# An attention and mixer kernel: three operations of the first steps moved, and one product put into another pair of banks

## The chip, the cores and the metric

The kernel runs on one core of a Trainium2 chip. A core has five engines that run side by side, each with its own queue of instructions taken in order: TensorE (PE in the profile: matrix products, with PEld for the loading of weights), VectorE (DVE), ScalarE (ACT), GpSimd (POOL) and SyncE (SP, which here only issues transfers). They wait for each other through semaphores. SBUF is the core's working memory, PSUM the memory that TensorE writes: eight banks of 2 KB in each of 128 partitions, used here in pairs. The metric is the device time of one execution, in microseconds (us).

## The reference

Linear attention with a decay for each head, in blocks of 64 positions, and then a mixing layer of low rank over the positions and a pair of large products over the channels. There are 4 batches, 8 heads, 768 positions, heads of 64 channels, hence 512 channels; the rank is 32 and the hidden width 2048.

```
for b in range(nb):                       # blocks of 64 positions
    intra = einsum('bhic,bhjc->bhij', qb, kb) * Dmask
    intra = einsum('bhij,bhjd->bhid', intra, vb)
    inter = einsum('bhid,bhde->bhie', qb * lam_pow, kv_state)
    out[:, :, sl] = intra + inter
    kv_state = lam_block * kv_state + einsum('bhsd,bhse->bhde', kb * rev_pow, vb)
x = out laid out as (batch, position, head * channel)
u = x + ((x^T U) V)^T                     # mixing over the 768 positions
result = u + relu(u @ w_ch1) @ w_ch2
```

q, k, v and lam come as 32-bit floating numbers. The four weights U, V, w_ch1 and w_ch2 come as 64-bit ones, and the kernel turns them into 32-bit ones on the chip, from pairs of 32-bit words. Its products that need more than one pass of TensorE use split operands: a high part, and what is left over (a low part).

## The kernel before

**Tiling.** The attention takes 128 positions at a time, all 8 heads at once: 6 such tiles for each of 4 batches, so 24 steps, s = 0 to 23, with c = s % 6 the tile's place in its batch. Behind them come the large products (from about 113 us), which hold most of the time; the change does not touch them.

**A step**, by the names of its parts, with the engine and line of each:

- `prep(s)`: TensorE turns q and k over (L419) into the pair of banks `pqk`, ScalarE copies them out as `qt` and `kt` (L425).
- `scale(s)`: GpSimd makes `qs`, q with its decay (L450), and then `ks` of the following step (L439).
- `scores(s)`: q by k on TensorE (L466), into `pss`.
- `masked(s)`: VectorE multiplies the scores by the mask of decays into `sm`, in two operations (L475).
- `intra(s)`: `sm` by v on TensorE (L524), into the pair `px`. Its first half waits for the first mask operation, the second half for the second.
- `inter(s)`: `qs` by the running state `kv` (L536), into the same `px`.
- `state(s)`: `ks` by v on TensorE (L489) into a part of a pair of banks that is called `pkv`; VectorE then makes the next state `kv` from it, by a copy at c = 0 (L495), and elsewhere by adding the faded old state (L497), which `fade(s)` made on ScalarE (L459).
- `take_x(s)`: ScalarE copies `px` out (L546), which frees `px`. There is one pair `px`, so the next step's first product into it waits for that.
- `next_v`, `next_k` and the loads in `prep` issue the loads of later tiles; `next_v` stands on ScalarE's queue.
- behind the sixth step of a batch, `low(b)` multiplies x by U (L556), `low_rows` splits the result into high and low parts, on VectorE (L589, L597) and GpSimd (L598), and four transfers on SyncE's queue exchange halves of it (L608).
- a batch later, `mix(s)` multiplies by V (L631) into the pair `pm`, `mixed(s)` adds the result to x on VectorE (L643), `turn` turns x over into the other columns of `pm` (L694), and ScalarE, VectorE and GpSimd split it for the large products (L708, L709, L701).

The pairs of banks are `pm`, `pss`, `pqk` and `px`: eight banks, all taken. A tile that goes into a pair waits until what was there before has been read.

**Order.** The order is written out by hand: one list `pieces` of (part, step), each part issuing its instructions on the queues of its engines, in the order of the list. On each engine the instructions run in that order. `aside(s)` is the place in step s at which the conversions of the weights stand; which of them stand there says the table that assigns the steps of `u_side`, `v_steps()` and `w1_steps` to places. `aside_first` says whether `aside(s)` stands ahead of `masked(s + 1)` or behind it. What a conversion has to do on ScalarE is kept back to the place `late`, in the following step.

**The conversions** of U and of V run through the same steps. `one`: VectorE takes out the exponent (L170) and the mantissa (L158), and ScalarE makes the scale from the exponent (L177, L178). `two`: the low word is added (L188). `three` and `four`: the sign is put in and the two are multiplied (L196, L201). For V there follow `five`, the high part (L788, and copies on ScalarE, L795), and `low`, the low parts of its rows: group 3 on GpSimd and group 1 on VectorE (L799). Each `low` is two operations, one for each half of the columns, 32 partitions by 384. At `aside(3)`, in the fourth step, stand the last two operations of U (L196, L201) and the first of V (L170, L158). At `aside(6)`, in the seventh step and behind `masked(7)`, stand both operations of V's low part on VectorE.

Of the kernel before, what the change touches and what calls it, by code (L numbers as in the profile page):

```python
# [18 lines left out]
def kernel(  # L19
# [28 lines left out]
    nc = tc.nc  # L48
# [3 lines left out]
    NT = S // P  # L52
# [36 lines left out]
    def on_scalar(what):  # L89
        if late and late[0] is None:  # L90
            late.append(what)
        else:
            what()
# [216 lines left out]
    def two_banks(name, tag):  # L310
        return psf.tile([P, 2, N], FP32, tag=tag, name=name)
# [7 lines left out]
    def bank(shape, name, tag):  # L319
        return psa[0].tile(shape, FP32, tag=tag, bufs=2, name=name)  # L320
# [5 lines left out]
    def parts(s):  # L326
        return 2 if s == 0 else 1
# [67 lines left out]
    half = [slice(0, D), slice(D, P)]  # L395
# [81 lines left out]
    def state(s):  # L477
        c = s % NT
        if c < NT - 1:
            ks, vr = st[s]["ks"], raw[s, "v"]  # L480
            if c == 0 and s > NT:
                pkv = st[s]["px"][:, 0, HP * D : 2 * HP * D]
            else:
                tag = "pm" if s <= NT else "pss" if c > 1 else "pqk"
                pkv = two_banks("pkv", tag)[:, 0, 0 : HP * D]
            pkv = pkv.rearrange("p (a e) -> p a e", a=HP)
            for a in range(HP):
                for x in range(2):
                    nc.tensor.matmul(  # L489
                        out=pkv[half[x], a, :], lhsT=ks[:, a, x, :], rhs=vr[:, 2 * a + x, :],  # L490
                        start=True, stop=True,
                    )
            kv[s + 1] = att.tile([P, HP, D], FP32, tag="kv", bufs=2, name="kv")
            if c == 0:
                nc.vector.tensor_copy(out=kv[s + 1], in_=pkv)  # L495
            elif "faded" in st[s]:
                nc.vector.tensor_tensor(out=kv[s + 1], in0=pkv, in1=st[s]["faded"], op=ALU.add)  # L497
            else:
                for a in range(HP):
                    nc.vector.scalar_tensor_tensor(  # L500
                        kv[s + 1][:, a, :], kv[s][:, a, :], lamc[:, a, :], pkv[:, a, :],
                        ALU.mult, ALU.add,
                    )
# [47 lines left out]
    def low(b):  # L551

        pp = two_banks("pp", "px")[:, 0, 0:P] if b < B - 1 else bank([P, P], "pp", "b2")
        for c in range(NT):
            for g in range(G):
                nc.tensor.matmul(  # L556
                    out=pp[g * R : (g + 1) * R, :], lhsT=u_w[:, c, :],
                    rhs=xs[b * NT + c][:, g * P : (g + 1) * P],
                    start=(c == 0), stop=(c == NT - 1),
                )  # L560
        pps[b] = pp
# [156 lines left out]
    for s in range(NS):  # L718
        b, c = divmod(s, NT)
        done = s - NT - 1  # L720
        more = s + 1 < NS
        turns = done > 0 and (done - 1) // TG < FG
        mixes = 0 <= done < NS - NT - 1
        rows = c == 0 and b > 0
        step = [("fade", s)] * (c > 0)
        step += [("mix", done)] * (mixes and c != 1) + [("turn", done - 1)] * turns
        step += [("next_of_low", b - 1)] * rows
        step += [("split", done - 1)] * turns
        step += [("prep", s + 1)] * more
        step += [("mix", done + 1)] * (not more)  # L730
        step += [("scale", s + 1)] * more
        step += [("mixed", done)] * (mixes and c != 1)
        step += [("late", s - 1)] * (1 < s < NT - 1 or s > NT)
        step += [("turned", done - 2)] * (done > 1 and c == 1)
        step += [("mixed", done + 1)] * (not more)
        both = [("intra", s), ("state", s)] 
        if s in inter_first:
            step += [("inter", s)] + both + [("next_v", s)]
        else:
            step += (both if s > NT else both[::-1]) + [("next_v", s), ("inter", s)]  # L740
        step += [("take_x", s)]
        step += [("next_of_low", b - 1)] * rows
        step += [("late", s)] * (s < 2 or s in (NT - 1, NT))
        step += [("turned", done - 1)] * (done > 0 and c > 0)
        step += [("mix", done), ("mixed", done)] * (mixes and c == 1)
        step += [("scores", s + 1)] * more
        step += [("low", b)] * (more and c == NT - 1)
        aside_first = 0 < s < NT - 2 or s > NT and c > 0
        step += [("aside", s)] * aside_first
        step += [("masked", s + 1)] * more  # L750
        step += [("low_rows", b)] * (more and c == NT - 1)
        step += [("aside", s)] * (not aside_first)
        step += [("store", done)] * (done >= 0 and done // TG < FG)
        step += [("next_k", s)] * (s > 0)
        pieces += step
    waiting = {name: list(range(NS)) for name in "qkv"}

    def load_next(name, engine=nc.sync):
        if waiting[name]:
            load(name, waiting[name].pop(0), engine)  # L760


    run = {
        "prep": prep, "fade": fade, "scores": scores, "masked": masked, "inter": inter, "take_x": take_x,
        "intra": intra, "state": state,
        "low": low, "low_rows": low_rows, "next_of_low": next_of_low, "mix": mix, "turn": turn,
        "mixed": mixed, "store": store, "next_v": next_v, "split": lambda s: splits.pop(s)(),
        
        "next_k": lambda s: load_next("k"), "third_v": lambda s: load_next("v", nc.scalar), "scale": scale, "turned": lambda s: turned.pop(s)(),
    }  # L770
    def v_steps():

        st = {}

        def dst():
            if "v" not in st:
                st["v"] = wconv.tile([P, C], FP32, tag="wf", name="vf")[0 : 2 * R, 0:SH]
            return st["v"]

        def parts(gs):  # L780
            for half in range(2):
                rows, cols = slice(half * R, (half + 1) * R), slice(half * SH, (half + 1) * SH)
                for g in gs:
                    yield v_hl[g * R : (g + 1) * R, cols], rows

        def five():
            st["t"] = t = wconv.tile([P, C], FP32, tag="wt", name="vt")[0 : 2 * R, 0:SH]
            nc.vector.tensor_scalar(  # L788
                t.bitcast(U32), st["v"].bitcast(U32), HI, None, ALU.bitwise_and
            )  # L790
            on_scalar(high)

        def high():
            for out, rows in parts((0, 2)):
                nc.scalar.copy(out, st["t"][rows])  # L795

        def low(g, engine):
            for out, rows in parts((g,)):
                engine.tensor_tensor(  # L799
                    out=out, in0=st["v"][rows], in1=st["t"][rows], op=ALU.subtract  # L800
                )

        halves = [moe_V[:, half * SH : (half + 1) * SH] for half in range(2)]
        return weight_steps(dst, halves, SH, 2 * R, in_parts=True) + [
            five, lambda: low(3, nc.gpsimd), lambda: low(1, nc.vector),
        ]


    u_side = weight_steps(
# [2 lines left out]
    side = {}  # L812
    for steps, at in (
        (u_side, (-1, 2, 2, 3, 3)),
        (v_steps(), (1, 1, 3, 4, 4, 4, 4, 5, 6)),
        (w1_steps(0, True, True), (8, 9, 10, 11, 12, 14, 15, 16, 17, 17, 20, 21)),
        (w1_steps(1, True, True), (14, 15, 16, 17, 18, 22, 23, NS, NS, NS, NS, NS)),
    ):
        assert len(steps) == len(at)
        for step, n in zip(steps, at):  # L820
            side.setdefault(n, []).append(step)
# [631 lines left out]
    for i in range(FT - EARLY, len(steps) - STAG):  # L1453
        g, ft = steps[i]
# [49 lines left out]
```

## Time and profile before

The time before is 637.38 us, the median of three runs (637.07 to 637.69).

| What | Value |
| --- | --- |
| time of the profiled execution | 637.08 us |
| its span, first to last instruction | 635.3 us |
| TensorE busy | 627.3 us, 99% |
| VectorE busy | 467.6 us, 74% |
| ScalarE busy | 330.9 us, 52% |
| GpSimd busy | 146.9 us, 23% |
| mean granted TensorE clock | 0.999 |

The page of the profile gives the busy time of each engine and "the chain of work that ended last", followed back from the last instruction to whatever released it, with the share of each engine. Other views of the same trace are used: the waits (which engine waited for which, in us, how many times, and the longest), and the timeline (start in us, duration in us, engine, line, operation, what it writes and reads, how many instructions the row merges, and in brackets the idle time before it and what ended it). A wait for several things is put down to the one that came last, and a name in brackets can be that of an engine that had long been done.

### The profile page before, as it was taken

How to read it: one execution, taken by the hardware profiler on the slowest of the kernel's cores; microseconds unless marked ns; L12 is line 12 of the kernel's file. 1: busy time of each engine (PE TensorE's matmuls, PEld its weight loads, DVE VectorE, ACT ScalarE, POOL GpSimd, SP SyncE). 2: the span in 40 equal slices, each digit the busy share in tenths (PEclk: the TensorE clock that was granted, in tenths of full speed). 3: DMA queues.
4: the chain of work that ended last, by engine and by line, in shares of the span. 5: the costliest groups of instructions: out<-in, count | busy, mean ns of one | idle time of the engine just before them, and what ended most of it. 6: DMA issues, size and time to landing. Idle time of an engine off the chain costs nothing.

```text
span 635.3 us, 13669 instructions
## 1 busy us (share of the span) xinstructions
PE 627.3 (99%) x5213; PEld 529.2 (83%) x5213; DVE 467.6 (74%) x752; ACT 330.9 (52%) x604; POOL 146.9 (23%) x125
## 2 busy tenths in 40 slices
PE   9999999999999999999999999999999999999997
PEld 8888989888888888888888888888888888888886
DVE  5776887757888788797888799784665754855844
ACT  4675756546777777778777744332322322323220
POOL 4476878000000000000667500030210300300300
PEclk9999999999999999999999999999999999999999
DMA  9989995348797888755876796363353353542521
GB/s 223 254 215 253 249 247 153 133 166 289 284 348 270 309 292 291 272 199 187 262 231 212 239 323 217 116 232 100 108 208 99 137 195 100 190 128 96 183 84 66
DMA packets 141955, 129.61 MB, mean 204 GB/s; under 512 B 82562, under 2 KB 99970, under 8 KB 141890
## 3 DMA queue, kind: packets, MB, share of 16 engines
q1 hardware_dynamic: 116768, 122.32, 59.6%
q10 hardware_dynamic: 25122, 6.42, 4.5%
q8 instruction: 41, 0.67, 0.4%
q14 instruction: 24, 0.20, 0.1%
HBM read 79.04 MB, written 49.28 MB: 202 GB/s over the span
## 4 chain that ended last, share of the span: by engine, by line
PE 97%; DVE 1%; ACT 1%; DMA 1%; issue 0%; ACTq 0%; DVEq 0%
PE pz L983 24%; PE pz L1343 14%; PE pz L1345 14%; PE pd L1347 14%; PE z L983 5%; PE pss L466 4%; PE px L524 4%; PE p L983 3%; PE pz L911 2%; PE d L983 2%; PE px L536 2%; PE pqk L419 2%; PE c L983 2%; PE pkv L489 1%; PE pd L922 1%; PE pp L556 1%
## 5 line engine op out<-in xcount | busy, mean ns | idle before, releaser
L1319 ACT ACTIVATE m<-rm 128x512 fp32r<-128x512 f32 x96 | 60.6, 631 | 174.0 <-PE pd L1347 131.0
L1324 DVE SCALAR_TENSOR_TENSOR m<-rm,m 128x512 fp32r<-128x512 f32 x96 | 71.6, 747 | 81.0 <-ACT m L1319 81.0
L983 PE MATMUL pz<-u_hl,w 128*128 128x512 f32 x448 | 110.3, 389 | 0.0
L1343 PE MATMUL pz<-w_hl,m 128*128 128x512 f32 x264 | 102.7, 389 | 0.0
L1345 PE MATMUL pz<-w_hl,m 128*128 128x512 f32 x264 | 102.7, 389 | 0.0
L1347 PE MATMUL pd<-w_d,m 128*128 128x512 f32 (+1 forms) x267 | 101.4, 387 | 0.0
L983 PEld LDWEIGHTS pz<-u_hl,w 128*128 128x128 f32 x448 | 84.1, 188 | 17.5
L285 POOL TENSOR_TENSOR w<-w 128x512 fp32r<-128x512 f32 x29 | 40.5, 1414 | 210.8 <-DVE w L279 197.3
L1325 DVE SCALAR_TENSOR_TENSOR m<-m 128x512 fp32r<-128x512 f32 x96 | 74.9, 780 | 3.1
L1375 POOL TENSOR_TENSOR o<-o,u 128x512 f32<-128x512 f32 x20 | 29.8, 1521 | 198.5 <-DVE o L1371 198.5
L983 PE MATMUL pz<-u_d,w 128*128 128x512 f32 x224 | 59.9, 389 | 0.0
L1347 PEld LDWEIGHTS pd<-w_d,m 128*128 128x128 f32 x267 | 49.8, 188 | 10.3
L1345 PEld LDWEIGHTS pz<-w_hl,m 128*128 128x128 f32 x264 | 49.6, 188 | 10.3
L1343 PEld LDWEIGHTS pz<-w_hl,m 128*128 128x128 f32 x264 | 49.6, 188 | 10.2
L983 PEld LDWEIGHTS pz<-u_d,w 128*128 128x128 f32 x224 | 42.0, 188 | 8.7
L1343 PE MATMUL pz<-w,m 128*128 128x512 f32 x120 | 46.7, 389 | 0.0
L1345 PE MATMUL pz<-w,m 128*128 128x512 f32 x120 | 46.7, 389 | 0.0
L1347 PE MATMUL pd<-w,m 128*128 128x512 f32 x120 | 46.7, 389 | 0.0
L990 ACT ACTIVATE pz<-pz 128x512 f32<-128x512 f32 x56 | 32.5, 581 | 26.4 <-PE pz L983 26.4
L475 DVE TENSOR_TENSOR sm<-pss,mask 128x512 f32<-128x512 f32 x48 | 30.9, 685 | 18.7 <-PE pss L466 18.4
L994 ACT ACTIVATE r<-pz 128x512 f32<-128x512 f32 x56 | 33.2, 595 | 12.1 <-PE pz L983 11.4
L196 DVE SCALAR_TENSOR_TENSOR sc<-words,sc 128x512 uint32<-128x512 uint32 (+2 forms) x34 | 23.7, 696 | 18.0 <-ACT sc L178 18.0
(140 smaller groups left out, 1119.8 us busy)
## 6 DMA issues: line engine op xcount, KB each, us to landing
r_d<-r SPq DMA_DIRECT2D x96, 256.0 KB, 2.9
rm<-r_d SPq DMA_DIRECT2D x96, 256.0 KB, 2.6
words<-in_moe_w_ch_dram SPq DMA_DIRECT2D x30, 512.0 KB, 5.1
wf<-forms_d SPq DMA_DIRECT2D x56, 128.0 KB, 2.9
u_d<-x_nat SPq DMA_DIRECT2D x24, 256.0 KB, 3.8
u<-u_d SPq DMA_DIRECT2D x24, 256.0 KB, 4.9
qraw<-in_q_dram SPq DMA_DIRECT2D x23, 256.0 KB, 5.0
out_dram<-o SPq DMA_DIRECT2D x23, 256.0 KB, 2.0
```

Source lines behind the costliest of these rows:

```text
L285: engine.tensor_tensor(out=st["third"], in0=st["low"].bitcast(FP32), in1=st["hi"].bitcast(FP32), op=ALU.subtract,)
L475: nc.vector.tensor_tensor(out=sm[:, x], in0=pss[:, x], in1=mask[:, x], op=ALU.mult)
L983: nc.tensor.matmul(out=out, lhsT=weights, rhs=moving, start=start and i == 0, stop=i == len(pieces) - 1, skip_group_check=not start,)
L990: nc.scalar.mul(acc, acc, 1.0 + E)
L994: nc.scalar.mul(r, acc, 4096.0)
L1319: nc.scalar.activation(out=m[:, 0], in_=rs[i], func=AF.Relu, scale=NEAR)
L1324: nc.vector.scalar_tensor_tensor(m[:, 1], r, 0.0, hi, ALU.max, ALU.subtract)
L1325: nc.vector.scalar_tensor_tensor(m[:, 2], hi, E, low, ALU.mult, ALU.subtract)
L1343: nc.tensor.matmul(out=pz, lhsT=m[:, 0, cols], rhs=hi, start=first, stop=False)
L1345: nc.tensor.matmul(out=pz, lhsT=m[:, 1, cols], rhs=low, start=False, stop=end)
L1347: nc.tensor.matmul(out=pd[:, part], lhsT=m[:, 2, cols], rhs=third[:, part], start=first, stop=end, skip_group_check=part.stop != C,)
L1375: nc.gpsimd.tensor_tensor(out=o, in0=o, in1=u, op=ALU.add)
```

## The change

Four edits.

- `aside_first` no longer holds for s = 3. In the fourth step U's last two operations and V's first two on VectorE stand behind `masked(4)`, no longer ahead of it.
- V's low part on VectorE is split. Its first operation, for the first half of the columns, stands in the seventh step (s = 6) behind `state(6)`, so ahead of `masked(7)`; the second stays at `aside(6)`, behind `masked(7)`.
- In the eighth step (s = 7) `state(7)` is issued ahead of `intra(7)`, not behind it.
- `state(7)` writes into the pair `pm`, which `mix(0)` takes next, no longer into `pqk`.

```diff
-                tag = "pm" if s <= NT else "pss" if c > 1 else "pqk"
+                tag = "pm" if s <= NT + 1 else "pss" if c > 1 else "pqk"
...
-        both = [("intra", s), ("state", s)] 
+        both = [("intra", s), ("state", s)] + [("v_low", s)] * (s == NT)
...
-            step += (both if s > NT else both[::-1]) + [("next_v", s), ("inter", s)]
+            step += (both if s > NT + 1 else both[1:] + both[:1]) + [("next_v", s), ("inter", s)]
...
-        aside_first = 0 < s < NT - 2 or s > NT and c > 0
+        aside_first = 0 < s < NT - 3 or s > NT and c > 0
...
-        def low(g, engine):
-            for out, rows in parts((g,)):
+        def low(g, engine, half=slice(0, 2)):
+            for out, rows in list(parts((g,)))[half]:
...
-            five, lambda: low(3, nc.gpsimd), lambda: low(1, nc.vector),
+            five, lambda: v_low.append(lambda: low(1, nc.vector, slice(0, 1))),
+            lambda: low(3, nc.gpsimd), lambda: low(1, nc.vector, slice(1, 2)),
...
+    v_low = []
+    run["v_low"] = lambda s: v_low.pop()()
...
-        (v_steps(), (1, 1, 3, 4, 4, 4, 4, 5, 6)),
+        (v_steps(), (1, 1, 3, 4, 4, 4, 4, 5, 5, 6)),
```

NT is 6, the number of tiles in a batch. No instruction is added or removed on any engine, and on ScalarE, GpSimd and SyncE the order stays as it was.

## The prediction, made before the changed kernel ran

> **What bounds the kernel now.** I read the page's chain first, then TensorE's waits, then the timeline of steps 2 to 8, engine beside engine. Steps are counted from s = 0: the "fourth step" is s = 3, the "eighth" is s = 7, and kv(s) is the state that inter(s) reads.
>
> The chain that ended last:
>
> ```profile
> PE 97%; DVE 1%; ACT 1%; DMA 1%; issue 0%; ACTq 0%; DVEq 0%
> ```
>
> TensorE is the path, so an edit is worth what it takes from TensorE's waits. These are the ones inside the attention steps (us in total, times, longest):
>
> ```profile
> PE px L524 <- issue: 1.1, 3, 0.6
> ...
> PE px L524 <- ACT qt L425: 0.7, 1, 0.7
> ...
> PE pm L631 <- DVE x_nat L643: 0.3, 1, 0.3
> ```
>
> The second is intra(4) at 25.44 us. The third is mix(1) at 41.44. Of the first, 0.35 us stands before intra(7) at 37.28. They add up to 1.3 us, 0.2% of the time, and that is nearly all the change can win. It is also about what a measurement of this kernel can tell from no change (0.2%, 1.27 us).
>
> The timeline around step 4, with step 2 ahead of it (start, duration, engine):
>
> ```profile
> 17.06 1.27 POOL L450 TENSOR_TENSOR qs<-qt,powq 128x512 f32<-128x512 f32 x1 [1.49 <-ACT qt L425]
> ...
> 17.40 1.05 DVE L170 TENSOR_SCALAR sc<-words 128x192 uint32<-128x192 uint32 x1
> ...
> 18.29 1.07 POOL L439 TENSOR_TENSOR ks<-kraw,small 128x512 f32<-128x512 f32 x1
> 18.37 1.11 DVE L158 TENSOR_SCALAR m<-words 128x192 uint32<-128x192 uint32 x1
> ...
> 22.46 1.16 PE L466 MATMUL pss<-qt,kt 64*128 64x128 f32 x16
> ...
> 23.28 0.36 DVE L196 SCALAR_TENSOR_TENSOR sc<-words,sc 128x192 uint32<-128x192 uint32 x1 [1.37 <-ACT sc L178]
> ...
> 24.06 0.35 DVE L170 TENSOR_SCALAR sc<-words 64x384 uint32<-64x384 uint32 x1
> ...
> 24.61 1.27 DVE L475 TENSOR_TENSOR sm<-pss,mask 128x512 f32<-128x512 f32 x2
> ...
> 25.38 1.28 POOL L450 TENSOR_TENSOR qs<-qt,powq 128x512 f32<-128x512 f32 x1 [2.11 <-ACT qt L425]
> ...
> 25.44 1.19 PE L524 MATMUL px<-vraw,sm 128*64 128x64 f32 x32 [0.71 <-ACT qt L425]
> ...
> 27.32 0.59 ACT L546 COPY x_nat<-px 128x512 f32<-128x512 f32 x1 [0.37 <-PE px L536]
> ...
> 28.76 0.69 PE L536 MATMUL px<-kv,qs 64*64 64x64 f32 x32
> ```
>
> See two things. The mask of step 4 (24.61) starts behind the conversions, although its scores began at 22.46 and a mask otherwise follows its scores by 1.21 (14.65 to 15.86, 27.18 to 28.39): it is 0.94 late, and intra(4) with it. And L170 takes 0.35 at 24.06, with GpSimd idle, for 384 elements, but 1.05 at 17.40 for 192, ending 0.12 behind GpSimd's operation (18.33). L158 behind it likewise ends 0.12 behind the next one. The two engines shut each other out.
>
> The timeline of steps 7 and 8:
>
> ```profile
> 36.49 1.29 DVE L475 TENSOR_TENSOR sm<-pss,mask 128x512 f32<-128x512 f32 x2 [1.00 <-PE pss L466]
> ...
> 37.32 1.05 POOL L439 TENSOR_TENSOR ks<-kraw,small 128x512 f32<-128x512 f32 x1
> ...
> 37.81 2.52 DVE L799 TENSOR_TENSOR vp<-vf,vt 32x384 fp32r<-32x384 f32 x2
> 38.34 1.58 POOL L450 TENSOR_TENSOR qs<-qt,powq 128x512 f32<-128x512 f32 x1
> ...
> 39.79 0.50 PE L631 MATMUL pm<-vp 64*128 64x256 f32 x4
> ...
> 40.36 0.42 DVE L497 TENSOR_TENSOR kv<-pkv,faded 128x256 f32<-128x256 f32 x1
> ...
> 41.44 0.50 PE L631 MATMUL pm<-vp 64*128 64x256 f32 x4 [0.26 <-DVE x_nat L643]
> ```
>
> V's two low parts take 2.52 us, each waiting for one GpSimd operation. They push back kv(8), then mixed(0), then mix(1).
>
> **Part A: the fourth step's conversions behind the mask.** The mask of step 4 moves to 22.46 + 1.21 = 23.67. Intra follows a mask by 0.79 (36.49 to 37.28), so it could start at 24.46. TensorE is then still in state(4) (24.04, 0.62 by the chain), so intra(4) starts at 24.66 and not 25.44: 0.78 won there.
>
> What is late next are the conversions. L196 goes to 23.67 + 1.21 = 24.88, L201 to 25.27, L170 to 25.66 (spacing 0.39, as at 23.28 to 24.06). GpSimd's qs(5) comes at 25.38 as before, since it waits for ScalarE's qt(5), which nothing here moves. L201, which reads two SBUF tiles, holds it off to about 25.5 (the first low half made the operation at 38.34 take 1.58 and not 1.27 in the same way); qs(5) then ends at 26.77. L170 waits for that and ends at 26.98 (0.12 as in step 2, 0.1 more for 384 elements). Then ks(6) runs to 27.9, and L158 ends at 28.1.
>
> Behind L170 stand ScalarE's two exponent operations of V (L177, L178: 0.65 and 0.62), ahead of take_x(4) on ScalarE's queue. They move from 25.68 to 27.02 and end at 28.29. An independent ScalarE copy starts 0.1 before the end of the one before (25.31 to 25.21), so take_x(4) goes from 27.32 to 28.2 and ends at 28.8. It frees px for inter(5), which follows by 0.05: 28.85 against 28.76. So A gives its 0.78 back and costs **+0.1**.
>
> Covers: kv(5) moves to 28.05 and ends at 28.47, before inter(5). The mask of step 5 starts at 28.4, as now (28.39). The load next_v(4), issued by ScalarE after L178 starts, goes from 26.67 to 27.8 and lands 3.9 later, at 31.7; its V is read in step 7, after 37, so 5 us cover it. GpSimd's ks(6) is read at 33.7. Bounds for A: -0.7 if L170 gets in before qs(5) (take_x then ends at 27.99, inter(5) starts at 28.04), +1.2 if it waits for ks(6) too. I take +0.1, because the row at 17.40 is the same line under the same two GpSimd operations.
>
> [...]
>
> **Part B: V's low part in two places, state(7) first, in pm.** In the old clock (A shifts all of it alike). The first half goes behind kv(7)'s copy (35.06), to 35.40. It costs 0.54 alone (L188, 64x384, at 29.60) and may wait for GpSimd's four subtractions, which end at 36.00: it ends between 35.9 and 36.45. The mask of step 7 starts at 36.49, so the half costs nothing; without that cover the mask would be late by up to its 0.54. It can put off GpSimd's fourth subtraction and qs(7) by 0.3. The fourth transfer of the exchange is issued at 36.65 behind the third anyway, and inter(7) needs qs(7) only at 38.67.
>
> State(7) runs at 36.97 to 37.59, in TensorE's 0.35 us wait; its pair pm is free since kv(7)'s copy ended (35.48). Intra(7) goes to 37.59, inter(7) to 38.67, and TensorE is ready for mix(0) at 39.29, against 39.79.
>
> The added wait: mix(0) writes the pair that state(7) filled, so it waits for kv(8), and kv(8) is queued behind the second low half. That half issues at 37.81, waits for ks(8), which now ends between 38.37 and 38.65, and ends 0.42 later (the first half before: 37.81 + 0.98, 0.42 behind ks). Kv(8) takes 0.03 and 0.42 more, release to TensorE 0.05 (41.38 to 41.44): mix(0) at 39.3 to 39.57. I take 39.5; the exchange's last transfer (36.65 + 2.7 = 39.35) is in by then. Behind mix(0) wait scores(8), +0.34 (39.79 to 40.13), and mix(1), +1.09: 40.93 against 41.44. Mixed(0), done by 39.5 + 0.47 + 0.68 = 40.65, no longer holds mix(1). **-0.5**, bounds -0.3 (39.57 and a tenth more) and -0.66 (only the transfer at 39.35 holds mix(0)). The mask of step 8 follows at 41.05, intra(8) could start at 41.84, and TensorE arrives at 42.1.
>
> **Sum.** The profiled execution took 637.08, its span 635.30 and 1.78 around it. +0.1 - 0.5 = -0.4, so 636.7; the median of the three runs is 0.30 above it: 637.38 - 0.4 = 637.0. From 42 us on TensorE waits for no other engine, so a shift there arrives at the end. The short "issue" waits (0.57 the longest, at 89.78) may fall otherwise, some 0.2 us either way.
>
> **Rivals.**
> - *No collision.* L170 slips in before qs(5). For it: L170 comes 0.28 after it, no more. Against: the row at 17.40. -0.7 - 0.5 = -1.2: 636.2. Chance 0.24.
> - *Slower by the pair of banks.* The second low half misses the gap behind ks(8) and waits for qs(8) too, as the second half does now: it ends at 40.33, kv(8) at 40.78, mix(0) starts at 40.83, mix(1) at 42.26: +0.8, with A +0.9, 638.3. B loses from the point where that half ends after 39.5; I expect 39.0. Against: at 37.81 the first half got in right behind ks. Chance 0.12.
> - *Slower by ScalarE.* L170 waits for qs(5) and ks(6), take_x(4) ends at 29.9: A +1.2, sum +0.7, 638.1. Against: at 17.40 L170 got in between the two. Chance 0.09.
>
> **Numbers.** The forecast has 0.55, its own range 636.6 to 637.4. Faster by over 0.2% (below 636.1): 0.14 of the first rival's 0.24 and 0.03 of the forecast, 0.17. Slower by over 0.2% (above 638.65): half of each slow rival, 0.06 and 0.05, 0.11. Within: 0.72. The range 636.0 to 638.2 leaves out about a tenth at either end.
>
> **What would show it.** Right: the mask of step 4 near 23.7, intra(4) near 24.7, L170 and L158 over 1 us each, take_x(4) near 28.2, a TensorE wait of some 0.8 us before inter(5) near 28.85; one low half before 36.5, the other ending near 39.0, mix(0) near 39.5 (+0.1), no wait before mix(1). Wrong: L170 at 0.35, inter(5) before 28.3, or a wait of over 0.5 us before mix(0).

## The result, and the profile after

The changed kernel took 640.35 us, the median of 6 runs (639.44 to 642.28), against 637.15 for the kernel before in the same session (636.2 to 637.69). The ratio is 1.0057 with a 95% interval of 1.0039 to 1.0076: **slower by 3.2 us**, outside the predicted range of 636.0 to 638.2, and more than the 0.2% that the prediction gave a chance of 0.11. A second session gave 642.21 against 638.36, 1.0065 [1.0045, 1.0086].

The profiled execution took 642.28 us, its span 640.5, at a mean granted clock of 0.996; it is the slowest of its six.

The chain that ended last in the changed kernel:

```profile
PE 96%; DMA 2%; DVE 1%; issue 0%; ACT 0%; POOL 0%; ACTq 0%; DVEq 0%; POOLq 0%
```

TensorE is still the path, with a point of its share gone to waits. These are its waits inside the attention (us in total, times, longest):

```profile
PE px L536 <- ACT x_nat L546: 1.7, 1, 1.7
PE pm L631 <- DMA vp<-vp: 1.5, 1, 1.5
...
PE pss L466 <- issue: 0.8, 1, 0.8
PE pp L556 <- issue: 0.4, 1, 0.4
PE px L524 <- issue: 0.4, 1, 0.4
PE pm L631 <- DVE kv L497: 0.3, 1, 0.3
```

Both waits that the change was aimed at are gone: intra(4) for the mask (0.7) and mix(1) for x (0.3). In their place stand inter(5), which waits 1.7 us for take_x(4); mix(0), which waits 0.3 us for kv(8) and then 1.5 us for the exchange; and a stop of 0.8 us inside scores(4) to which the profile gives no releaser.

The timeline of the changed kernel around the mask of step 4 (start, duration, engine):

```profile
22.74 0.93 PE L466 MATMUL pss<-qt,kt 64*128 64x128 f32 x10
24.43 0.60 PE L466 MATMUL pss<-qt,kt 64*128 64x128 f32 x5 [0.76 <-issue]
...
25.18 1.29 DVE L475 TENSOR_TENSOR sm<-pss,mask 128x512 f32<-128x512 f32 x2 [3.40 <-PE pss L466]
...
26.38 0.35 DVE L196 SCALAR_TENSOR_TENSOR sc<-words,sc 128x192 uint32<-128x192 uint32 x1
26.39 1.47 POOL L450 TENSOR_TENSOR qs<-qt,powq 128x512 f32<-128x512 f32 x1 [3.76 <-ACT qt L425]
26.77 1.31 DVE L201 SCALAR_TENSOR_TENSOR u_w<-m,sc 128x192 f32<-128x192 f32 x1
...
27.82 2.30 POOL L439 TENSOR_TENSOR ks<-kraw,small 128x512 f32<-128x512 f32 x2
28.11 1.09 DVE L170 TENSOR_SCALAR sc<-words 64x384 uint32<-64x384 uint32 x1
29.13 1.21 DVE L158 TENSOR_SCALAR m<-words 64x384 uint32<-64x384 uint32 x1
...
29.24 0.61 ACT L177 ACTIVATE sc<-sc,vp 64x384 f32<-64x384 uint32 x1 [2.43 <-DVE sc L170]
29.89 0.62 ACT L178 ACTIVATE sc<-sc,vp 64x384 uint32<-64x384 f32 x1
...
30.26 0.41 DVE L497 TENSOR_TENSOR kv<-pkv,faded 128x256 f32<-128x256 f32 x1
30.41 0.56 ACT L546 COPY x_nat<-px 128x512 f32<-128x512 f32 x1
...
31.07 0.69 PE L536 MATMUL px<-kv,qs 64*64 64x64 f32 x32 [1.66 <-ACT x_nat L546]
```

Read it from the bottom. Inter(5) waits for take_x(4), which follows L178 and L177 on ScalarE. ScalarE sat idle for 2.43 us ahead of L177, until L170 was done on VectorE. L170 is late because it stands behind L201, and three conversions in a row (L201, L170, L158) took over 1 us each, where they took 0.35 each before. In that time GpSimd ran qs(5), from 26.39, and its two operations for the keys behind it, from 27.82. Kv(5), which inter(5) reads too, was done at 30.67, just 0.3 us ahead of the end of take_x(4). And the mask itself, forecast for 23.67, is at 25.18, behind the scores that stopped.

Steps 7 and 8 of the changed kernel:

```profile
38.54 0.55 DVE L799 TENSOR_TENSOR vp<-vf,vt 32x384 fp32r<-32x384 f32 x1
39.64 1.29 DVE L475 TENSOR_TENSOR sm<-pss,mask 128x512 f32<-128x512 f32 x2 [0.55 <-PE pss L466]
40.96 1.24 DVE L799 TENSOR_TENSOR vp<-vf,vt 32x384 fp32r<-32x384 f32 x1
42.23 0.42 DVE L497 TENSOR_TENSOR kv<-pkv,faded 128x256 f32<-128x256 f32 x1
...
42.71 0.38 PE L631 MATMUL pm<-vp 64*128 64x256 f32 x1 [0.33 <-DVE kv L497]
44.59 0.64 PE L631 MATMUL pm<-vp 64*128 64x256 f32 x3 [1.50 <-DMA vp<-vp]
44.82 1.91 PE L466 MATMUL pss<-qt,kt 64*128 64x128 f32 x15
```

The first low half is ahead of the mask and in its cover, as forecast. Counted from the start of the mask of step 7, the second half ends at 2.56 us (forecast 2.51) and mix(0) starts at 3.07 (forecast 3.01). Then three of its four products wait for the exchange, and scores(8) takes 1.91 us where it takes 1.16 elsewhere. The windows say why (stretch, its length, busy time and number of instructions of TensorE, its weight loads, VectorE, ScalarE and GpSimd; the third column from the right is the granted clock):

```profile
42.00:44.00 2.00, 0.76 (x29) 0.42 (x19) 0.62 (x2) 1.54 (x5) 2.00 (x2) 1.00 0.79 179
44.00:46.00 2.00, 1.41 (x14) 1.41 (x16) 0.69 (x1) 0.00 (x0) 0.34 (x1) 0.70 0.97 217
46.00:48.00 2.00, 2.00 (x31) 2.00 (x29) 1.03 (x2) 0.18 (x1) 0.00 (x0) 0.50 0.54 158
48.00:50.00 2.00, 2.00 (x62) 1.86 (x60) 1.55 (x3) 1.49 (x3) 0.74 (x1) 0.95 0.70 159
```

Right behind the wait TensorE runs at half its clock, 0.50 from 46 to 48 us. The loss of clock adds up to 2 x (0.30 + 0.50 + 0.05) = 1.7 us, that is 3.4 us at half. In the kernel before no window from 16 to 60 us is below 1.00. This half clock is in no sentence of the prediction.

Where the time went, in one table: the time from one take_x to another (starts of L546, in us), for the kernels told of below. In the first profile of the changed kernel take_x(9) is 5.8 us later than in the kernel before, and the last, take_x(23), 5.2: steps 4 to 8 hold the loss.

| Kernel | 3 to 5 | 5 to 6 | 6 to 8 | half clock before 60 us |
| --- | --- | --- | --- | --- |
| before | 7.71 | 4.82 | 9.10 | no |
| changed, first profile | 10.43 | 5.65 | 11.78 | 44 to 50 |
| changed, second profile | 9.63 | 6.82 | 8.58 | no |
| second edit alone (x_low) | 8.27 | 4.81 | 8.74 | no |
| third edit alone (x_state) | 8.02 | 5.21 | 11.50 | 42 to 48 |
| first edit alone (x_aside) | 10.31 | 6.04 | 8.98 | 30 to 36 |
| x_aside and products in the gap (x_busy) | 10.33 | 5.91 | 8.99 | no |
| x_aside, exponents later (x_late) | 9.26 | 4.84 | 9.01 | no |
| x_late, V's two behind kv(5) (x_kv) | 8.27 | 5.13 | 10.06 | no |
| V's two alone behind the mask (x_v) | 8.84 | 4.94 | 9.21 | no |
| second and third edits (x_lowstate) | 8.63 | 5.07 | 11.55 | 42 to 48 |
| the same, second profile (ls_again) | 7.55 | 5.06 | 8.04 | no |
| changed, exponents later (full_late) | 9.92 | 5.49 | 11.74 | 46 to 50 |

Each row is a single execution. The kernel before has only one profile, and kernels that share its order up to step 5 (x_low, x_state, x_lowstate, ls_again) take 7.55 to 8.63 from take_x(3) to take_x(5), so a difference of half a microsecond in that column says little.

### The profile page after: what moved, and what is told of

It reads as the page before. It is cut to its first block, busy times and chain, and to the rows that moved or that the text cites. A ratio compares the mean times of both kernels' runs of the same rounds, so it can differ in the third digit from the quotient of the medians.

```text
span 640.5 us, 13669 instructions
## 1 busy us (share of the span) xinstructions
PE 630.0 (98%) x5213; PEld 531.8 (83%) x5213; DVE 471.8 (74%) x752; ACT 330.9 (52%) x604; POOL 147.1 (23%) x125
## 4 chain that ended last, share of the span: by engine, by line
PE 96%; DMA 2%; DVE 1%; issue 0%; ACT 0%; POOL 0%; ACTq 0%; DVEq 0%; POOLq 0%
PE pz L987 24%; PE pz L1349 14%; PE pz L1347 14%; PE pd L1351 14%; PE z L987 5%; PE pss L466 4%; PE px L524 4%; PE p L987 3%; PE pz L915 2%; PE d L987 2%; PE px L536 2%; PE c L987 2%; PE pqk L419 2%; PE pkv L489 1%; PE pd L926 1%; PE pm L631 1%
## 5 line engine op out<-in xcount | busy, mean ns | idle before, releaser
L196 DVE SCALAR_TENSOR_TENSOR sc<-words,sc 128x512 uint32<-128x512 uint32 (+2 forms) x34 | 23.5, 690 | 16.3 <-ACT sc L178 16.3
```

## The experiments

All were timed beside the kernel before on the same chip; a ratio is to the runs of the kernel before in the same session (medians 637.02 for the first four, 637.14 for the second four, 638.36 for the third four, 638.07 for the last three). The theories change as the runs come in; each expectation stands as it was written. State(7) first and its place in `pm` belong together and are called the third edit here.

### One part at a time

The first edit alone (`x_aside`):

```diff
-        aside_first = 0 < s < NT - 2 or s > NT and c > 0
+        aside_first = 0 < s < NT - 3 or s > NT and c > 0
```

> The first edit alone: in the fourth step the conversions of U and V stand behind the mask of step 4. The changed kernel's profile has TensorE idle for 1.66 us before inter(5), behind ScalarE's take_x(4), which stood behind V's exponents, which waited for L170 under GpSimd's operations. Theory 1 (the conversions collide with GpSimd and hold take_x(4) back) expects +1 to +2 us, with a wait of 1 us or more before inter(5). The prediction's step A expects +0.1 and a wait of 0.8. Theory 2 (the loss is the late exchange before mix(0)) expects between -0.7 and +0.3.

Measured: 641.39 us (640.59 to 643.47), 1.0068 [1.0050, 1.0087]. The first edit alone loses 4.4 us, so it is enough for the whole loss; theory 1 had +1 to +2. In its profile inter(5) waits 0.87 us, behind a stop of 0.62 us in the transposes, so the wait that theory 1 wanted to see (1 us or more) is there only if both are counted.

The split of V's low part alone (`x_low`): `v_low` in the seventh step, as in the change, without the edits of `tag` and of the order at s = 7.

> The second edit alone: V's first low half ahead of the mask of step 7, the second behind it. Theory 2 (that half holds up GpSimd's fourth subtraction, so the exchange's last transfer is issued and lands late, and mix(0) waits for it) expects +0.5 to +1.5 us and a wait for the exchange before mix(0). Theory 1 expects a gain, -0.2 to -0.6: only one of the two low parts is left in front of kv(8).

Measured: 636.47 us, 0.9999 [0.9981, 1.0018]: no difference that can be measured. The interval, 1.2 us to either side, leaves room for the smaller values of both theories; mix(0) doesn't wait for the exchange in its profile, which speaks against theory 2.

State(7) first and in `pm`, alone (`x_state`):

```diff
-                tag = "pm" if s <= NT else "pss" if c > 1 else "pqk"
+                tag = "pm" if s <= NT + 1 else "pss" if c > 1 else "pqk"
...
-            step += (both if s > NT else both[::-1]) + [("next_v", s), ("inter", s)]
+            step += (both if s > NT + 1 else both[::-1]) + [("next_v", s), ("inter", s)]
```

> The third edit alone: state(7) ahead of intra(7) and in the pair pm, both low halves still behind the mask of step 7. Mix(0) must then wait for kv(8), which stands behind both low halves (40.36 to 40.78 in the old clock): mix(0) at 40.83 and mix(1) at 42.26, against 39.79 and 41.44, so +0.8 by the rows of before. Theory 1 and theory 2 expect the same here, since neither touches this; a gain would say that neither the pair nor the queue counts.

Measured: 638.54 us, 1.0024 [1.0009, 1.0039]: slower by 1.5. Mix(0) waits 1.48 us for kv(8), which is queued behind both low halves. So the split is what makes state(7) first bearable. In six of its twelve runs the mean granted clock was 0.996 or 0.997; the other six, at 0.999 or 1.000, average 637.94, which is 0.7 above the kernel before (mean 637.23), close to the 0.8 expected.

Both together, without the first edit (`x_lowstate`):

> The second and third edits together, without the first. The prediction's step B expects -0.5 us. Theory 1 (the loss is the conversions') expects -0.5 to 0 and so nearly all of the loss of 3.2 us gone. Theory 2 (the exchange) expects +0.5 to +2.5, mix(0) waiting for the exchange.

Measured: 637.22 us, 1.0003 [0.9988, 1.0018]. Nearly all of the loss is gone without the first edit, as theory 1 had it. A gain of 0.5 us doesn't show, though the interval still holds it (0.9992). Its profile is that of its slowest run (641.4), with 1.28 us of waiting for the exchange and the half clock behind it.

### The chain through ScalarE, the queue of VectorE, and the clock

L177 and L178 of the fifth step behind take_x(4), added to the first edit (`x_late`), and alone (`b_late`):

```diff
-        step += [("late", s - 1)] * (1 < s < NT - 1 or s > NT)
+        step += [("late", s - 1)] * (1 < s < NT - 2 or s > NT)
...
-        step += [("take_x", s)]
+        step += [("take_x", s)] + [("late", s - 1)] * (s == NT - 2)
```

> First edit alone, as in x_aside (641.4), and V's two exponent operations on ScalarE (L177 and L178) moved from ahead of take_x(4) to behind it in the fifth step. Theory 1 (the chain: the last collision holds L170 to 28.6, L177 and L178 come next on ScalarE, take_x(4) is queued behind them to 30.4, inter(5) waits for it, and the idle of TensorE then brings the half clock): the chain is cut, inter(5) comes by 29.2 and is no longer the end of a wait for take_x(4), no half clock behind it; 637.0, between 636.2 (the 0.78 of the earlier mask kept) and 637.5. Rival 1b (the collisions themselves: VectorE and GpSimd lose 1 us each time, and the copy of kv(5), mask(5) and the keys are late by it whatever ScalarE does): it stays between 639 and 641.5.

> The kernel before, with nothing but L177 and L178 of the fifth step moved behind take_x(4). In the kernel before take_x(4) at 27.32 waited 0.37 us for inter(4), not for ScalarE, and inter(5) at 28.76 followed the transposes without a gap: so all theories expect no difference, 637.0 (636.7 to 637.3). It shows what of x_late's time is the move's own.

Measured: x_late 638.39 us, 1.0014 [1.0003, 1.0025]; b_late 636.99 us, 0.9991 [0.9981, 1.0001]. Three of the 4.4 us go when take_x(4) no longer stands behind L177 and L178, and none of x_late's twelve runs is at a mean granted clock below 0.999. That is neither the 637.0 of theory 1 nor the 639 and more of rival 1b. Around inter(5) in x_late:

```profile
27.79 0.59 ACT L546 COPY x_nat<-px 128x512 f32<-128x512 f32 x1 [1.10 <-PE px L536]
...
29.30 0.41 DVE L497 TENSOR_TENSOR kv<-pkv,faded 128x256 f32<-128x256 f32 x1
...
30.07 0.69 PE L536 MATMUL px<-kv,qs 64*64 64x64 f32 x32
```

The rest, 1.25 us, is more than I expected to stay: the collisions are as before (L201 1.31, L170 1.10), and the sum that makes kv(5) comes at 29.30, 3.5 us later than in the kernel before.

V's two operations alone behind the mask, U's two ahead of it (`x_v`):

```diff
-        (v_steps(), (1, 1, 3, 4, 4, 4, 4, 5, 6)),
+        (v_steps(), (1, 1, -3, 4, 4, 4, 4, 5, 6)),
...
-        step += [("aside", s)] * (not aside_first)
+        step += [("aside", s)] * (not aside_first) + [("aside", -3)] * (s == 3)
```

> In the fourth step only V's two VectorE operations (L170, L158) go behind the mask; U's two (L196, L201) stay ahead of it as in the kernel before. Theory 1 (the chain): with nothing ahead of it L170 waits for GpSimd's qs(5) at most, not for qs(5) and ks(6) both; it ends by 27.0 instead of 28.6, take_x(4) begins by 28.3, inter(5) by 28.9 against 28.76 in the kernel before: 637.0, between 636.3 and 637.8. Rival 1b (each operation put behind the mask costs its own collision): half of the loss stays, about 639.

Measured: 637.52 us, 1.0001 [0.9991, 1.0011]. The timeline of x_v on VectorE behind the mask:

```profile
25.04 1.29 DVE L475 TENSOR_TENSOR sm<-pss,mask 128x512 f32<-128x512 f32 x2 [1.14 <-PE pss L466]
26.25 0.34 DVE L170 TENSOR_SCALAR sc<-words 64x384 uint32<-64x384 uint32 x1
26.51 1.43 DVE L158 TENSOR_SCALAR m<-words 64x384 uint32<-64x384 uint32 x1
```

The first operation behind the mask gets in beside qs(5), which starts at 26.25 as well, and takes 0.34. The second waits for qs(5). Here the first is L170 and the second is L158, for which nobody waits in a hurry; in the changed kernel the first is L196, and L170 is the third. X_v has fewer collisions too, so by itself it doesn't tell their number from their place. X_late does: there L201 and L170 collide as in x_aside, and 3.1 us of the loss go once take_x(4) no longer stands behind L170's exponent. So most of the cost is what hangs on the operation that a collision falls on.

V's two moved on, behind the sum that makes kv(5), added to x_late (`x_kv`):

```diff
+            step += (both if s > NT else both[1:] + [("aside", -3)] * (s == 4) + both[:1]) + [("next_v", s), ("inter", s)]
```

> x_late (638.4) with V's two operations L170 and L158 moved on, behind VectorE's sum that makes kv(5) (L497); U's two stay behind the mask. Theory 1c (what is left of the loss in x_late is kv(5): L497 is queued behind operations that wait for GpSimd, 29.30 there against 25.81 before, and inter(5) reads kv(5)): L497 begins by 28.2, inter(5) no longer waits for it, 637.1 (636.4 to 637.7). Rival (what is left is something else, such as the stalls of TensorE to which the profile gives no releaser): 638.4 as x_late.

Measured: 638.67 us against 638.36, 1.0007 [0.9990, 1.0023]. No loss that can be measured is left: 0.3 us where x_late has 1.25. L497 starts 2.84 us behind the mask of step 4, against 4.23 in x_late. That points to the queue of VectorE ahead of kv(5) as the second way in which the first edit loses, but doesn't settle it. The two intervals (1.0003 to 1.0025 and 0.9990 to 1.0023) overlap, and in both profiles inter(5) follows the transposes, which had a stop of their own (0.62 and 0.34 us); in the table most of the difference of x_late and x_kv is before take_x(4). Where the wait for kv(5) does show is in full_late, below.

Three extra products of the identity, 128x128, in front of inter(5) in x_aside (`x_busy`; their result is not read):

```diff
+            step += [("filler", s)] * (s < NT)
...
+    def filler(s):
+        out = two_banks("idle", "pm")[:, 0]
+        for i in range(3):
+            nc.tensor.matmul(out=out[:, 0:P], lhsT=ident, rhs=ident, start=True, stop=True)
```

> First edit alone, as in x_aside (641.4), and three extra 128x128 products of the identity by itself, whose result nobody reads, on TensorE ahead of inter(5), where x_aside had TensorE idle for 0.87 us (and for 0.62 us a microsecond before that). Theory of the clock (the idle before inter(5) brings a stretch of some 3.4 us at half clock, worth about 2 us): no window at 0.5 between 30 and 36 us, 639.4. Rival (the half clock has another cause, or isn't worth 2 us): the windows show 0.5 as before and the time stays at 641.4 or goes up by 0.3.

Measured: 640.76 us, 1.0050 [1.0033, 1.0067]. No window of its profile is below 1.00, as the theory of the clock said, and one of its eight runs was at the lower clock, against three of six in x_aside; but the time is 1.4 above what the theory gave. The products waited 0.75 us for kv(5), whose old banks they use, so they shortened the idle stretch only a little (0.34 + 0.75 us for 0.62 + 0.87), and they pushed inter(5) on by some 0.6 themselves. So this experiment neither settles what brings the half clock nor gives its price. Single runs say more of the price. A run's mean granted clock is either 0.996 to 0.997 (once 0.993) or 0.999 to 1.000:

| Kernel | runs at the lower clock | their mean | mean of the others | difference |
| --- | --- | --- | --- | --- |
| before, all sessions | 1 of 117 | 640.01 | 637.72 (its session) | 2.3 |
| changed, first session | 2 of 6 | 642.03 | 639.98 | 2.1 |
| changed, second session | 3 of 6 | 642.83 | 641.79 | 1.0 |
| x_aside | 3 of 6 | 642.09 | 641.13 | 1.0 |
| x_state | 6 of 12 | 639.76 | 637.94 | 1.8 |
| x_lowstate | 1 of 12 | 641.40 | 637.13 | 4.3 |
| ls_again | 4 of 12 | 638.97 | 637.41 | 1.6 |
| full_late (below) | 6 of 12 | 643.15 | 639.88 | 3.3 |
| v_late (below) | 2 of 12 | 641.01 | 637.46 | 3.5 |
| x_busy | 1 of 8 | 641.94 | 640.46 | 1.5 |
| b_shift (below) | 1 of 8 | 642.79 | 639.52 | 3.3 |
| x_low, x_late, x_v, b_late, x_kv, best | 0 of 71 | | | |

So a run at the lower clock is 1.0 to 4.3 us longer than the others of its kernel. That holds the idle stretch ahead of the half clock as well; the half clock itself takes 1.7 us by the windows of each profile that has it. It comes in 5 of the changed kernel's 12 runs: 0.4 of 1.7, or 0.7 us of the mean. It adds to the loss and isn't its base; without it x_aside still stands at 641.13 against a mean of 637.23, 3.9 us above.

### The whole kernel

The whole change with L177 and L178 behind take_x(4) (`full_late`), and the changed kernel once more (`again`):

> The whole change, and L177 and L178 of the fifth step behind take_x(4), as in x_late. Theory 1 (most of the loss of the whole change is the chain through ScalarE to take_x(4)): x_late took 3.0 us off x_aside (641.39 to 638.39), so 640.35 less 3.0, 637.3 (636.7 to 638.4), and take_x(4) begins no more than 1 us later than in the kernel before. Rival (in the whole kernel the loss is mostly the wait of mix(0) for the exchange and the half clock behind it): 639.4 or more.

> The changed kernel once more, for more runs and a second profile. All theories: 640.4 (639.9 to 641.0); take_x(4) some 3 us later than in the kernel before. Theory of the exchange (mix(0)'s wait for it is part of every execution of this order): the wait of 1.5 us at L631 is there again. Rival (it belonged to the slowest execution alone): under 0.5 us.

Measured: full_late 640.80 us, 1.0038 [1.0017, 1.0059]; again 642.21 us, 1.0065 [1.0045, 1.0086]. Against its own session each, the cut chain is worth 1.4 us in the whole kernel, and 3.1 in x_aside. So theory 1 doesn't carry over: full_late stays 2.4 us above the kernel before, as its rival had it (639.4 or more, where the kernel before took some 637). In the profile of full_late, its slowest run, take_x(4) is only 0.7 us later than in the kernel before (counted from take_x(3)), as forecast, but inter(5) then waits 1.41 us for kv(5), and mix(0) 1.38 us for the exchange, with the half clock behind it. This run, 6.4 us above the median, also has the longest waits of any profile behind 60 us (1.39 us at 96, 2.66 at 105). Six of its twelve runs had the lower clock; the other six average 639.88, 1.4 above the mean of the kernel before (638.47). The second profile of the changed kernel has the delay before inter(5) again (1.65 us), a stop of 1.60 us in L556, and no wait at all for the exchange, so that wait isn't part of every execution.

The second and third edits once more (`ls_again`), the earlier mask without its chain (`v_late`: x_v and b_late together), and what cost nothing alone (`best`: x_low and b_late together):

> The second and third edits without the first, as x_lowstate, once more, for more runs and another profile. Theory 3 (the prediction's step B: take_x(7) comes 0.6 earlier and mix(0) follows it): a ratio of 0.9992, take_x(8) no later than in the kernel before, counted from take_x(6). Theory 2 (the exchange or the half clock takes it back): 1.0003 or more, and in the profile take_x(8), counted from take_x(6), over 1 us later than in the kernel before.

> V's two operations L170 and L158 behind the mask of the fourth step, U's two ahead of it, and L177 and L178 of the fifth step behind take_x(4): the earlier mask with no chain hung on it. If the earlier mask is worth something (0.35 us for each operation moved, 0.7 in all): 0.9985, about 636.2 where the kernel before takes 637.1. If the stop of TensorE in scores(4) takes it (the mask waits for the last of scores(4), which the stop of 0.2 to 1.4 us delays by as much as the conversions did): 1.0000.

> The two edits that cost nothing alone: L177 and L178 of the fifth step behind take_x(4) (b_late, 0.9991) and the low half of V in two places (x_low, 0.9999), without the others. All theories: 0.9990, some 0.6 us below the kernel before; if the sum shows nothing, 1.0000.

Measured: ls_again 638.10 us against 638.07, 1.0005 [0.9991, 1.0019]; v_late 637.48, 1.0001 [0.9984, 1.0019]; best 637.47, 0.9995 [0.9980, 1.0011]. None is faster than the kernel before by what can be measured; the intervals of v_late and best still hold the gains that were thought possible (0.9985 and 0.9990). Ls_again's profile, though, is that of a run in which all went as step B of the prediction had it; steps 7 and 8 of it:

```profile
36.58 1.29 DVE L475 TENSOR_TENSOR sm<-pss,mask 128x512 f32<-128x512 f32 x2
37.90 0.68 DVE L799 TENSOR_TENSOR vp<-vf,vt 32x384 fp32r<-32x384 f32 x1
38.61 0.42 DVE L497 TENSOR_TENSOR kv<-pkv,faded 128x256 f32<-128x256 f32 x1
...
39.16 0.50 PE L631 MATMUL pm<-vp 64*128 64x256 f32 x4
...
40.46 0.50 PE L631 MATMUL pm<-vp 64*128 64x256 f32 x4
```

The second half takes 0.68, mix(0) follows inter(7) without a wait, and mix(1) follows scores(8). Take_x(8) comes 8.04 us behind take_x(6), 1.06 less than before, and the run took 635.63.

What takes that back in the profiles that lose is the exchange. SyncE took 2.78 to 3.26 us to issue its four transfers in ten profiles, and TensorE then never waited for them. In the seven where it took 3.56 to 3.90, mix(0) waited 0.94 to 1.50 us for them in five; of the other two, x_state waited 1.48 us for kv(8) and x_aside for neither. The five are three of the five profiles with the second and third edits in place, and two others (x_kv 0.94, and best, which has the second alone, 1.18). So the longer issue isn't the edits' own, but with mix(0) forecast 0.5 earlier there is less to cover it, and the half clock follows: in each of the three, and in neither of the two others. What makes the issue longer stays open. The delay stands in one of the four transfers: its issue takes 1.53 to 1.86 us in each of the seven, where the longest takes 0.75 in the kernel before. How often the exchange is late in the runs without a profile isn't known. In x_lowstate only one run of twelve was at the lower clock, and the other eleven are no faster than the kernel before (means 637.13 and 637.23), so the half clock doesn't explain there why the gain is missing.

### The stops inside TensorE's work

The kernel before with four more 16x16 products at the start (`b_shift`):

```diff
-    keep_busy(3 + 8)
+    keep_busy(3 + 8 + 4)
```

> The kernel before with four more of the 16x16 products on TensorE at the start (8 matmul records more). In most profiles so far scores(4) stops after its 10th of 16 records for 0.2 to 1.4 us, and the next such stops come 128 records on, in the transposes of the seventh step after 7 of 8, and then in L556. Theory of code loading (TensorE's instructions arrive in blocks, so the stops have fixed places in its stream): the stop in scores(4) moves by 8 records to after the 2nd of 16, if there is one, and none is after the 10th. Rival (something of scores(4) itself is waited for): it stays after the 10th. The time is that of the kernel before in both, 637.0 and up to 0.4 more.

Measured: 639.79 us, 1.0024 [1.0005, 1.0043]. The timeline of scores(4) in b_late, where TensorE's stream is that of the kernel before:

```profile
23.05 0.93 PE L466 MATMUL pss<-qt,kt 64*128 64x128 f32 x10
24.69 0.60 PE L466 MATMUL pss<-qt,kt 64*128 64x128 f32 x5 [0.71 <-issue]
```

And in b_shift:

```profile
24.12 0.49 PE L466 MATMUL pss<-qt,kt 64*128 64x128 f32 x2
...
26.03 1.04 PE L466 MATMUL pss<-qt,kt 64*128 64x128 f32 x13 [1.42 <-issue]
```

The stop moved by exactly the eight records: from behind the 10th to behind the 2nd. Its place is a place in TensorE's stream, not something that scores(4) waits for. Counting records, the next stops come 125 or 126 further on (not 128): in the transposes of step 6 behind the 7th of 8 (125 in x_low, x_late, x_v and x_kv), then in L556 behind the 37th (251 from scores(4) in both profiles of the changed kernel and in full_late), and in x_busy, with six records more ahead of it, behind the 31st (126 from the transposes). An estimate from the page of the kernel before: it lists a queue of kind "instruction" with 41 packets, and TensorE has 5213 products and as many loads of weights. If all of these came through that queue, a packet would hold 10426 / 41 = 254 of them, or 127 products, close to the 125 and 126 counted. No run shows that the queue is TensorE's, or that a stop is a wait for a packet of it.

I had expected at most 0.4 us of loss; it was 1.4. In its profile the stop in scores(4) is 1.42 us long, too long for the conversions to cover, and take_x(5) comes 9.37 us behind take_x(3). The profile has two more long stops, of 1.12 us at 65 us and 1.27 at 90, so the stop in scores(4) need not be the whole loss. Why it is longer at that place is open.

## Why the prediction was wrong

**Part A, +0.1 forecast, +4.4 measured (x_aside).** Two of its steps failed, and a third was missing.

The first is the 0.78 won at intra(4). It took scores(4) for done 1.16 us after its start, so that the mask starts at 1.21. It starts at 2.44 and 2.34 in the two profiles of the changed kernel, at 1.61 in x_aside and at 2.16 in x_late, against 2.15 before. The stop inside scores(4) shows as a row of 0.20 to 1.37 us, at the same record, in 12 of the 16 profiles with the unshifted stream, but not in the one that I had. The conversions had been standing in its cover. That the earlier mask is worth nothing fits v_late and x_v (1.0001 both), which move two of the four conversions; x_v's interval begins at 0.9991, v_late's at 0.9984, so up to 0.6 or 1.0 us is not excluded.

The second is "L201, which reads two SBUF tiles, holds it off". I held qs(5) at its old time while I moved the mask forward. Both follow scores(4): when that stops, the transposes and the copy of qt(5) behind it are late too, and qs(5) starts 1.20 to 1.22 us after the start of the mask in each of the six profiles of kernels with all four operations right behind it, where I had 1.71. That is the moment at which the first conversion, L196, gets in; so L201 loses to qs(5), L170 to the keys of step 6, and L158 to those of step 7 or to nobody. In the first profile of the changed kernel these three take 1.31, 1.09 and 1.21 us, for 0.35 or 0.36 in the kernel before, and L201 ends 0.22 us behind qs(5) (28.08 and 27.86). Which operation pays hung here on 0.4 us of scores: already in x_aside, where the mask starts 1.61 us behind scores(4) and not 1.21, qs(5) comes with L196. In each of the six L170 ends 4.02 to 4.04 us behind the start of the mask, where the sum had 3.31.

What followed was the rival "slower by ScalarE": L170 waits for the end of a second GpSimd operation, take_x(4) is late, and inter(5) with it. It had 0.09 and a price of +1.2 for A. The runs put 3.1 us on this chain with all that follows it (x_aside less x_late), and 0.9 more, with the doubt told above, on the queue ahead of kv(5) (x_late less x_kv, each against its own session). I had kv(5) end at 28.47, "before inter(5)"; it was 30.67 in the changed kernel. So two things hold inter(5) back at nearly the same time, and cutting one alone leaves the other, as full_late shows. The price is larger than the delay of inter(5) (2.3 us in the first profile). From take_x(5) to take_x(6) those profiles lose 0.8 to 2.0 us more: a half clock in x_aside, a stop in L556 in the two profiles of the changed kernel and in x_busy. In profiles with inter(5) on time L556 has no such row; it takes 1.52 to 2.04 us there, so a stop of 0.5 at most. Why it is longer behind a late inter(5) is open.

The third, missing, is the clock: no term and no rival spoke of the granted clock of TensorE, which stood at half for some 3.4 us behind idle stretches of 1.48 to 1.83 us in five profiles. It is worth some 0.7 us of the mean loss, by the 5 of 12 runs and the 1.7 us above.

**Part B, -0.5 forecast, no gain measured (x_lowstate 1.0003, ls_again 1.0005, each with an interval that still holds 0.9992).** In the profiles of the changed kernel the mechanism was right to a tenth of a microsecond: the low halves, kv(8), the pair `pm`, mix(0) at 3.07 us behind the mask of step 7 for 3.01, and no wait before mix(1). What failed is "the exchange's last transfer is in by then", at 2.86 us behind that mask. In the first profile of the changed kernel it was 4.95, in the second TensorE didn't wait for it. The slack that I took from one profile (0.15 us) is smaller than the spread of the issue, 2.78 to 3.90. The two profiles without the wait gain 0.5 and 1.1 us from take_x(6) to take_x(8), the three with it lose 2.4 to 2.7, the half clock included; the twenty-four runs of x_lowstate and ls_again show no difference.

**The sum.** Forecast 637.0 for 637.38 before; measured 640.35 for 637.15. Of the miss of 3.6 us, A alone would make 4.3 and B 0.7 by x_aside and x_lowstate; they add up to more than the miss, and the intervals of these runs, about 1 us to either side, leave room for that. The chance of 0.11 for slower by over 0.2% came from two cases in which one wait moves; here the stop, the collisions and the clock came together.

## What to carry to other kernels

Where operations of two engines are reordered that hold each other up, as VectorE's and GpSimd's did here, follow not how many collide but which operation comes to stand second and third, and what hangs on it: here 0.35 us operations became 1.1 to 1.4 us ones in both orders, and it cost nothing that can be measured when the exponent came first of two (x_v) and 4.4 us when it came third of four (x_aside). A wait that one profile shows as clean gain can be the cover of a stop that another execution has: the stop in scores(4) is absent from the one profile of the kernel before and stands in 12 of the 15 other profiles with the same stream up to there. And where TensorE is the path, an idle stretch of a microsecond and a half can cost twice, once itself and once in the clock behind it: in five profiles stretches of 1.48 to 1.83 us had another 1.7 us of lost clock behind them, and three stretches of 1.60 to 1.66 us had none.

## What the runs showed of the hardware that was not expected

- **The clock fell after short idles, and not each time.** The half clock stood in five profiles, each time with the same loss of 1.7 us in the windows (3.4 us at 0.50), and behind idle stretches of TensorE of 1.5 to 1.8 us, counted together where a few products stand between (0.33 + 1.50 in the changed kernel, 0.33 + 1.38 in full_late, 0.33 + 1.28 in x_lowstate, 0.62 + 0.87 in x_aside, 1.48 in x_state). It didn't come after 1.65 us before inter(5) or 1.60 us in L556 in the second profile of the changed kernel, nor after 1.66 us before inter(5) in the first. So the three idles without it, 1.60 to 1.66 us, lie inside the range of those with it, 1.48 to 1.83; what decides was not shown.
- **TensorE stopped at the same places of its stream in many profiles,** 125 or 126 records apart by the three places that were counted, for 0.2 to 1.6 us, and not in every execution: the place in scores(4) has a row of its own in 12 of 16 profiles. Four tiny products more at the start moved it by eight records (b_shift, 1.4 us slower, 1.0024 [1.0005, 1.0043]).
